# The first stage of an adaLN transformer block: modulation sums moved to the tensor engine, and a new order of the first lists

## The chip, the cores and the metric

The kernel runs on one core of one Trainium2 chip. The metric is the device time of one execution in microseconds (us). Engines are named as the profile names them: PE is the tensor engine (PEld its weight loads), DVE the vector engine, ACT the scalar engine, POOL the GpSimd engine, and SP the engine whose queue issues the transfers between device memory and the chip's SBUF. PSUM is the memory that PE writes its sums to; it is used here in banks of 512 float32 columns.

## What is computed

A block with adaptive layer norm: one conditioning row c gives six modulation rows, two of which (a shift `sa` and a scale `1 + ca`) act on the normalised input of the attention. The inputs are x (2048 rows of 576), c (one row of 576), `w_mod` (576 by 3456), the attention's `wqkv` and `wo`, and the feed-forward weights `w1` and `w2`, all float32. There are 32 heads of 18, and the feed-forward layer has 4608 columns.

```
mod = (silu(c) @ w_mod).reshape(1, 6, 1, 576)
sa, ca, ga, sb, cb, gb = (mod[:, i] for i in range(6))
h = layernorm(x) * (1 + ca) + sa
x = x + ga * attention(h, wqkv, wo)     # 32 heads of 18
h = layernorm(x) * (1 + cb) + sb
x = x + gb * (silu(h @ w1) @ w2)
```

## The kernel before

**Numbers in two parts.** Each large float32 product is computed from operands that are split into a high part (`fp32r`) and the rest, the low part. A product is made of three passes, high times high, high times low and low times high, for each of the four full slices of 128 of the 576 columns (kt 0 to 3). The last 64 columns (kt 4) hold the high part in one half of the partitions and the low part in the other, so two passes do there. This makes 14 matmuls for one sum; the names `hTh`, `hTl` (the transposed, modulated h), `wqh`, `wql` (a slice of the weights of q or k) and `wv` (those of v) are such parts.

**Two stages.** `start_tasks` writes the first stage, which ends at about 157 us in the profile; a planned main part follows with the attention and the feed-forward layer. The first stage is a list scheduler: each piece of work is a `Task` with an engine (P for PE, A for ACT, V for DVE, G for POOL, D for a transfer on SP's queue), an assumed duration, the tasks it depends on, a priority, and the buffers of rings that it takes and frees. `Start.run` steps through an assumed time and lets each free engine take the ready task of the smallest priority. The order in which tasks are taken is the order in which the instructions are written to each engine's queue; on the chip each queue runs strictly in that order, and each instruction waits for the data it needs.

**What the first stage does.** The rows of x come in 16 tiles of 128, in four groups of four (g 0 to 3). For a group: the tiles are loaded (`x_load`, L1368, 576 columns each, in a ring of eight buffers `xt`); `stats` takes mean and variance on DVE (L434, L435); `rstd_a`, `rstd_b` and `rstd_c` make the reciprocal deviation for the four tiles together, with a power on POOL (L1391) and five small operations on DVE (L1396 to L1400); `apply` normalises the tile in place on ACT (L1405); `dup` copies its last 64 columns once more behind the 576 on POOL (L1408), so that the fifth slice is 128 wide; `T` transposes slice kt of the four tiles on PE into one PSUM bank `psT` (L1413, four transposes), out of a ring of three banks; `out_T` reads the bank on ACT and applies scale and shift (`mod_out`, L459) into an SBUF tile `etmp`; `mod_hi` rounds `etmp` to the high part on DVE (L462, the CAST); `mod_lo` subtracts to the low part on POOL for even kt and on DVE for odd (L466, L468).

Then come the products: `single` (L1479) writes the 14 matmuls of one sum, in three parts of 6, 6 and 2. For k and q of a group (`psqk`, 512 columns) ACT takes the high part out of PSUM (L666) and DVE the low (L670), and both are stored to device memory (`kscr`, `qscr`); for v (`psv`, 288 columns) ACT copies the sum into `vst` (L1532), which is stored to `vscr`. Singles take turns on two PSUM banks, the rings f and v. Later products of the stage are written in pairs (`pair`, L539).

**The modulation.** c is loaded to all 128 partitions as a row, and silu(c) is made of it into `sbc` (L1355 on ACT, L1356 and L1357 on DVE). `w_mod`'s first two column blocks come transposed as five tiles `wm` of 128 by 1152 (`wf_load`, L1361). For each tile t, `mod_dot` takes two dot products with `sbc` on DVE (L567, 576 columns each, with the sum read out after each) and adds 1 to the scale (L572). The results stand in `modc`, one column for each t and kind; `out_T` of slice kt needs the two columns of t = kt. `aux` hands out one of three PSUM banks of the ring a; in the first stage it is used for the slots of the attention that are computed ahead (L890).

**Weights.** The weights of k and q come through a ring `raw` of two buffers, are rounded on ACT (L621) and subtracted on POOL (L626); the five tiles of v's weights come through the same ring (L616), are rounded on ACT (L1451) and subtracted on POOL (L1460), and take the buffers `wm` of the modulation when these are free.

## Time and profile before

| what | value |
|---|---|
| time, median of 3 runs | 2353.95 us (2350.65, 2353.95, 2354.07) |
| profiled execution, its own time | 2355.56 us |
| its span | 2353.8 us |
| PE busy in the span | 2293.4 us, 97% |
| DVE, ACT, POOL busy | 75%, 63%, 30% |
| first matmul starts | 17.63 us |
| first stage's last product, PE | 157.1 us |

The profile is of one execution. The difference of 1.8 us between its time and its span lies outside what the trace shows. A row of the timeline gives the start, the duration, the engine, the line, the operation with its output and inputs, and, in brackets, how long the engine was idle before and who released it. "x17" stands for 17 instructions in a row.

### The profile page before, as it was taken

The page shows a single profiled execution, that of the slowest core. Times are in us where ns is not written, and L with a number is a line of the kernel's source. Part 1 is how long each engine was busy: PE and PEld are TensorE (multiplying, and loading weights), DVE is VectorE, ACT ScalarE, POOL GpSimd, SP SyncE. Part 2 cuts the span into 40 slices and gives each one's busy share as a digit, 9 for nine tenths or more (in the row PEclk, how much of TensorE's full clock was granted, in tenths as well). Part 3 has the DMA queues.
Part 4 walks back from the last instruction along what each step waited for, and adds up shares of the span by engine and source line. Part 5 has one row for each costly group of instructions (what it writes and reads, how often), then busy time and mean ns, then how long its engine had stood idle before and what let it go on. Part 6 is the DMA issues. An engine that isn't in the chain of part 4 may idle for free.

```text
span 2353.8 us, 52121 instructions
## 1 busy us (share of the span) xinstructions
PE 2293.4 (97%) x19844; PEld 1580.8 (67%) x19844; DVE 1768.1 (75%) x3089; ACT 1473.9 (63%) x2710; POOL 712.2 (30%) x873
## 2 busy tenths in 40 slices
PE   5999999999899999999999999999999999999999
PEld 4874444444576767776677777776677767678998
DVE  7768899997788888877888878878887787344333
ACT  4337777776477777766677777766777677732221
POOL 5103333315656666675211111112211111110000
PEclk9999999999899999999999999999999999999999
DMA  7465555546456666666555555554645554345653
GB/s 243 154 194 175 168 168 168 184 151 209 157 192 219 222 222 214 218 207 227 206 171 171 183 176 167 166 181 141 224 165 164 194 184 174 115 152 196 221 201 114
DMA packets 201474, 433.01 MB, mean 184 GB/s; under 512 B 31362, under 2 KB 67618, under 8 KB 201226
## 3 DMA queue, kind: packets, MB, share of 16 engines
q1 hardware_dynamic: 201226, 429.68, 55.1%
q8 instruction: 158, 2.59, 0.5%
q14 instruction: 90, 0.74, 0.1%
HBM read 338.54 MB, written 86.33 MB: 181 GB/s over the span
## 4 chain that ended last, share of the span: by engine, by line
PE 86%; DVE 6%; DMA 3%; ACT 2%; issue 1%; POOL 1%; SPq 0%; DVEq 0%; ACTq 0%; POOLq 0%
PE ps L539 26%; PE psv L979 18%; PE psa L890 14%; PE ps L533 10%; PE psb L942 8%; PE psqk L654 3%; DVE mx L892 2%; PE psv L539 2%; DMA qt<-qscr 1%; PE psp L539 1%; PE psv L1479 1%; DMA raw<-in_w 1%; PE psqk L539 1%; PE psqk L1479 1%; PE psp L533 1%
## 5 line engine op out<-in xcount | busy, mean ns | idle before, releaser
L892 DVE TENSOR_REDUCE mx<-psa 128x1 f32<-128x512 f32 x2048 | 1329.2, 684 | 293.4 <-PE psb L942 165.2
L944 ACT ACTIVATE pt<-psb 128x512 f32<-128x512 f32 x2048 | 1148.4, 599 | 477.5 <-PE psb L942 303.8
L942 PE MATMUL psb<-qt,kb 56*128 56x512 f32 x2048 | 744.9, 421 | 3.5 <-ACT pt L944 3.5
L890 PE MATMUL psa<-ka,qt 54*128 54x512 f32 x2016 | 734.4, 418 | 11.9 <-DVE mx L892 9.3
L890 PEld LDWEIGHTS psa<-ka,qt 54*128 54x128 f32 x2016 | 348.6, 186 | 306.3 <-DVE mx L892 170.1
L979 PE MATMUL psv<-pt,vt 128*32 128x512 f32 x4096 | 510.1, 604 | 0.3 <-ACT ov L983 0.3
L539 PE MATMUL ps<-w2t,g 64*128 64x288 f32 x4992 | 412.5, 293 | 3.0 <-POOL w2t L775 1.6
L539 PEld LDWEIGHTS ps<-w2t,g 64*128 64x128 f32 x4992 | 384.4, 185 | 44.1 <-DVE x L1096 6.0
L942 PEld LDWEIGHTS psb<-qt,kb 56*128 56x128 f32 x2048 | 352.2, 186 | 26.4 <-ACT pt L944 15.7
L539 PE MATMUL ps<-hh,w1t 64*128 64x512 f32 x1944 | 352.9, 395 | 0.0
L1241 POOL TENSOR_TENSOR g<-etmp,g 128x512 fp32r<-128x512 f32 x108 | 137.4, 1292 | 386.6 <-ACT g L1240 349.4
L979 PEld LDWEIGHTS psv<-pt,vt 128*32 128x32 f32 x4096 | 102.3, 109 | 210.6 <-issue 202.5
L539 PEld LDWEIGHTS ps<-hh,w1t 64*128 64x128 f32 x1944 | 194.8, 186 | 43.1 <-ACT etmp L1237 3.4
L1103 POOL TENSOR_TENSOR x<-x,gt 128x288 f32<-128x288 f32 x116 | 93.1, 802 | 385.8 <-ACT gt L1102 385.4
L539 PE MATMUL ps<-hl,w1t 64*128 64x512 f32 x864 | 177.7, 392 | 0.0
L1096 DVE TENSOR_TENSOR x<-ps,x 128x288 f32<-128x288 f32 x184 | 83.3, 453 | 106.5 <-PE ps L533 71.5
L533 PE MATMUL ps<-w2t,g 128*128 128x288 f32 x960 | 130.8, 296 | 2.9 <-POOL g L1241 1.4
L533 PEld LDWEIGHTS ps<-w2t,g 128*128 128x128 f32 x960 | 128.6, 188 | 5.6 <-POOL g L1241 1.9
L1237 ACT ACTIVATE eq<-ps 128x512 f32<-128x512 f32 x36 | 21.6, 600 | 146.3 <-PE ps L533 146.3
L533 PE MATMUL ps<-hh,w1t 128*128 128x512 f32 x360 | 106.8, 390 | 0.5 <-DVE hh L468 0.5
L539 PEld LDWEIGHTS ps<-hl,w1t 64*128 64x128 f32 x864 | 88.8, 187 | 15.0
L1238 DVE SCALAR_TENSOR_TENSOR etmp<-etmp 128x512 f32<-128x512 f32 x108 | 74.6, 730 | 12.1 <-ACT etmp L1237 11.2
(150 smaller groups left out, 2138.8 us busy)
## 6 DMA issues: line engine op xcount, KB each, us to landing
w1t<-w1s SPq DMA_DIRECT2D x108, 640.0 KB
w2t<-w2s SPq DMA_DIRECT2D x108, 576.0 KB
kb<-kscr SPq DMA_DIRECT2D x512, 108.0 KB
ka<-kscr SPq DMA_DIRECT2D x504, 108.0 KB
w1s<-w1t SPq DMA_DIRECT2D x36, 640.0 KB
w2s<-w2t SPq DMA_DIRECT2D x36, 576.0 KB
vt<-vscr SPq DMA_DIRECT2D x32, 608.0 KB
qt<-qscr SPq DMA_DIRECT2D x128, 108.0 KB
```

The costliest lines, as they stand in the source:

```text
L533: mm(self.ps[late], lhsT=lhsT, rhs=rhs, start=(i == 0), stop=(i == self.n - 1))
L539: done = mm(self.ps[g], lhsT=lhsT[rows], rhs=rhs[rows], start=(s == 0), stop=(s == self.end))
L654: mm(qk_ps[0], lhsT=w[b][:, kt, :], rhs=(hTl if a else hTh)[:, kt, n * 512:(n + 1) * 512], start=(i == 0), stop=(i == 13))
L890: mm(ps, lhsT=t["q"][64 * j:64 * j + 54, hp, stt * P:(stt + 1) * P], rhs=t["a" if ("a", kc, hp) in t else "b", kc, hp][64 * j:64 * j + 54, ...
L892: return lambda: nc.vector.tensor_reduce(t["mx"][:, 2 * j + hp, stt, kc:kc + 1], ps, axis=AX.X, op=ALU.max)
L942: state["pe"] = mm(ps, lhsT=t["b", kt // 4, hp][64 * e:64 * e + 56, kt % 4 * P:(kt % 4 + 1) * P], rhs=t["q"][64 * e:64 * e + 56, hp, :], s ...
L944: nc.scalar.activation(t["P"][kt, hp][:, e, :], ps, AF.Exp, scale=SCALE)
L979: mm(t["ps"][32 * h:32 * h + 32, :], lhsT=t["v"][:, c0:c0 + 32], rhs=t["P"][kt, h // 2][:, h % 2, :], start=(kt == 0), stop=(kt == NKT - 1 ...
L1096: nc.vector.tensor_add(c["x1"][j][:, hs], ps, c["x1"][j][:, hs])
L1103: nc.gpsimd.tensor_add(c["x1"][j][:, hs], c["x1"][j][:, hs], t)
L1238: nc.vector.scalar_tensor_tensor(t, t, 1.0, u, op0=ALU.add, op1=ALU.mult)
L1241: (nc.vector if last else nc.gpsimd).tensor_tensor(g[:, 1, :], t, f(g[:, 0, :]), op=ALU.subtract)
```

## The change

- silu(c) is also made as a column: a small input `ccol` (128 by 6) is loaded first, and three small operations make `sc` of it. The row `sbc`, which the main part uses, is still made, but late (priorities 8.7 and 9).
- The ten dot products on DVE are gone. `mod_sum(t)` writes ten plain float32 matmuls of one column each on PE (five for the shift, five for the scale), with 128 by 128 slices of `w_mod` as weights, into a bank `psd` of the ring a. `mod_put(t)` is one small DVE operation that adds 0 and 1 to the two columns and stores them to `modc`. `w_mod`'s five tiles are laid out anew on the host; their size is the same.
- The high part of h is taken straight from the PSUM bank: `mod_hi_ps` is a DVE operation with scale and shift that reads `psT`, beside ACT's `out_T`, which reads it too. The CAST from `etmp` is gone. The low part waits for both.
- x is stored with its last 64 columns doubled, 640 wide. The copies on POOL are gone; loads and `apply` are 640 wide. Two of group 0's four `apply` are on DVE (`apply_v`).
- Singles take turns over the rings f, a, v, a: five banks in place of two. v's weights have a ring `rv` of four buffers of their own. The low parts of all weights wait, in the list, for group 0's norm.
- The list's rules change: some DVE tasks carry a flag `port`, and such a task and a task of POOL are not taken together; `RATE` is 340e3 for 320e3; transfers begin at 1.3. Several priorities and durations change.

```diff
-    RATE = 320e3
+    RATE = 340e3
+    FIRST = 1.3
...
+                if t.port and at <= now:
+                    held = min(held, t.prio)
+                at = max(at, free[t.eng], port if t.eng == "G" else free["G"] if t.port else 0.0)
...
+                if t.port and free["G"] > now or e == "G" and (port > now or t.prio > held):
+                    continue
+                if e == "V" and not t.port and t.prio > held and now + t.dur > free["G"] + 0.3:
+                    continue
...
+    def mod_hi_ps(kt, hi_dst, ps):
+        nc.vector.tensor_scalar(hi_dst, ps, modc[:, 1, kt:kt + 1], modc[:, 0, kt:kt + 1], op0=ALU.mult, op1=ALU.add)
...
-    def dot(w, dst):
-        return nc.vector.scalar_tensor_tensor(w, w, 1.0, sbc, op0=ALU.mult, op1=ALU.mult, accum_out=dst)
-
-    def mod_dot(i, t_, w):
-        ins = dot(w, modc[:, i, t_:t_ + 1])
-        if i % 2:
-            nc.vector.tensor_scalar_add(modc[:, i, t_:t_ + 1], modc[:, i, t_:t_ + 1], 1.0)
-        return ins
...
+        t = dma(20e3, lambda: nc.sync.dma_start(cc, ccol), prio=0)
+        t = add("A", 1.5, lambda: nc.scalar.activation(sc, cc, AF.Tanh, scale=0.5), [t])
+        t = add("V", 0.15, lambda: nc.vector.scalar_tensor_tensor(sc, sc, 1.0, cc, op0=ALU.add, op1=ALU.mult), [t], 0)
+        sc_t = add("V", 0.15, lambda: nc.vector.tensor_scalar_mul(sc, sc, 0.5), [t], 0)
...
+        def mod_sum(t_):
+            ps = d["ms", t_] = aux([P, 512], "psd")
+            for i in range(2):
+                for n in range(KT):
+                    c0, k_ = (256 * n + P * i, n) if n < 4 else (1024, 4 + i)
+                    mm(ps[:, i:i + 1], lhsT=d["wf", t_][:, c0:c0 + P], rhs=sc[:, k_:k_ + 1], start=(n == 0), stop=(n == KT - 1))
+
+        def mod_put(t_):
+            nc.vector.tensor_tensor(modc[:, 0:2, t_], d["ms", t_][:, 0:2], onec, op=ALU.add)
...
-            dots.append([add("V", 0.95 + 0.15 * i, lambda i=i, t_=t_: mod_dot(i, t_, d["wf", t_][:, i, :]), [t, sbc_t], 3, free=k) for i in range(2)])
+            k, ka = tok("wm"), tok("a")
+            t = dma(590e3, lambda t_=t_: wf_load(t_), prio=2 + 0.01 * t_, take=k)
+            t = add("P", 1.2, lambda t_=t_: mod_sum(t_), [t, sc_t], 3, take=ka, free=k, mode="full")
+            dots.append([add("V", 0.15, lambda t_=t_: mod_put(t_), [t], 1.5, free=ka)])
...
-            a_ = [add("A", 0.8, lambda i=4 * g + j: apply(i), [t], p - 0.5) for j in range(4)]
-            d_ = [add("G", 0.3, lambda i=4 * g + j: dup(i), [a_[j]], p - 0.5) for j in range(4)]
+            a_ = [add("A", 0.8, lambda i=4 * g + j: apply(i), [t], p - 0.5) if g or j % 2 == 0 else
+                  add("V", 0.58, lambda i=4 * g + j: apply_v(i), [t], 1.9) for j in range(4)]
...
-                hi = add("V", 0.6, lambda g=g, kt=kt: mod_hi(hl(g, kt)[0], d["e", g, kt]), [t], p - 0.4)
+                hi = add("V", 0.72, lambda g=g, kt=kt: mod_hi_ps(kt, hl(g, kt)[0], d["T", g, kt]), [tT] + dots[kt], p - 0.4, free=kb)
...
-            ring = "fv"[count[0] % 2]
+            ring = RINGS[count[0] % len(RINGS)]
```

The order of the instructions, at the places where it matters below. First PE, from its first instruction: `psT` are group 0's transposes, `psqk` its product of k, `psd` the new sums. Before:

```order
L1413 MATMUL psT<-ident,xt 128x128 x20
L1479 MATMUL psqk<-hTh,wqh 128x512
L1479 MATMUL psqk<-hTh,wql 128x512
L1479 MATMUL psqk<-hTl,wqh 128x512
L1479 MATMUL psqk<-hTh,wqh 128x512
L1479 MATMUL psqk<-hTh,wql 128x512
L1479 MATMUL psqk<-hTl,wqh 128x512
L1479 MATMUL psv<-wv,hTh 128x288 x2
```

and after:

```order
L1383 MATMUL psd<-sc,wm 128x1 x30
L1439 MATMUL psT<-ident,xt 128x128 x12
L1383 MATMUL psd<-sc,wm 128x1 x10
L1439 MATMUL psT<-ident,xt 128x128 x8
L1383 MATMUL psd<-sc,wm 128x1 x10
L1511 MATMUL psqk<-hTh,wqh 128x512
L1511 MATMUL psqk<-hTh,wql 128x512
L1511 MATMUL psqk<-hTl,wqh 128x512
```

The five groups of ten sums stand among the transposes of group 0, all ahead of the first product; the products of k and q now run one behind the other, and those of v, which stood between the parts of k, come after both.

Then DVE, from the last small operation of group 0's norm (`nm`) on. Before:

```order
L1400 SCALAR_TENSOR_TENSOR nm<-mv,rs 128x4
L567 SCALAR_TENSOR_TENSOR wm,modc<-wm,sbc 128x576 x2
L572 TENSOR_SCALAR modc<-modc 128x1
L567 SCALAR_TENSOR_TENSOR wm,modc<-wm,sbc 128x576 x2
L572 TENSOR_SCALAR modc<-modc 128x1
L567 SCALAR_TENSOR_TENSOR wm,modc<-wm,sbc 128x576 x2
L572 TENSOR_SCALAR modc<-modc 128x1
L462 CAST hTh<-etmp 128x512
L567 SCALAR_TENSOR_TENSOR wm,modc<-wm,sbc 128x576 x2
L572 TENSOR_SCALAR modc<-modc 128x1
```

and after:

```order
L1425 SCALAR_TENSOR_TENSOR nm<-mv,rs 128x4
L1386 TENSOR_TENSOR modc<-psd,onec 128x2
L1434 TENSOR_SCALAR xt<-xt,rs,nm 128x640 x2
L1386 TENSOR_TENSOR modc<-psd,onec 128x2 x2
L475 TENSOR_SCALAR hTh<-psT,modc 128x512 x3
L1386 TENSOR_TENSOR modc<-psd,onec 128x2
L475 TENSOR_SCALAR hTh<-psT,modc 128x512
L482 TENSOR_TENSOR hTl<-etmp,hTh 128x512
L1386 TENSOR_TENSOR modc<-psd,onec 128x2
L475 TENSOR_SCALAR hTh<-psT,modc 128x512
```

Eight of the ten dot products stood here behind the norm, with the first CAST among them; now there are five additions of two columns (`modc<-psd`), which wait for PE, two normalisations, and the high parts from `psT`.

Last POOL, from the power of group 0's norm to the first low parts. Before:

```order
L1391 TENSOR_TENSOR r_175<-ve,mhalf 128x4
L626 TENSOR_TENSOR wql<-raw,wqh 128x640
L1460 TENSOR_TENSOR wv<-raw,wv 128x576
L1408 COPY xt<-xt 128x64 x4
L1460 TENSOR_TENSOR wv<-raw,wv 128x576
L466 TENSOR_TENSOR hTl<-etmp,hTh 128x512
L1460 TENSOR_TENSOR wv<-raw,wv 128x576
```

and after:

```order
L1416 TENSOR_TENSOR r_183<-ve,mhalf 128x4
L633 TENSOR_TENSOR wql<-raw,wqh 128x640
L482 TENSOR_TENSOR hTl<-etmp,hTh 128x512 x2
L633 TENSOR_TENSOR wql<-raw,wqh 128x640
L484 TENSOR_TENSOR hTh<-etmp,hTh 64x512
L1492 TENSOR_TENSOR wv<-rv,wv 128x576 x2
L1416 TENSOR_TENSOR r_395<-ve,mhalf 128x4
```

The four copies and the low parts of v's weights are gone from between the norm and the low parts of h; v's come behind them.

From the last v products of the first stage on, PE's order is the same in both kernels, and behind the first stage the other engines differ by one or two rows that change places.

## Rows read from the trace of the kernel before

**Rows 1.** Windows by stretch: start, end, length, busy time by engine (instructions), clock, DMA.

```profile
core 0: us, PE busy (x) PEld busy (x) DVE busy (x) ACT busy (x) POOL busy (x), PEclk, DMA share, GB/s
0.00:5.00 5.00, 0.00 (x0) 0.00 (x0) 0.06 (x1) 1.28 (x1) 1.11 (x10) 1.00 0.58 118
5.00:17.60 12.60, 0.00 (x0) 0.00 (x0) 10.91 (x28) 3.08 (x5) 4.38 (x4) 1.00 0.97 356
17.60:25.10 7.50, 6.68 (x23) 4.85 (x23) 7.36 (x19) 6.31 (x9) 6.46 (x7) 1.00 0.78 263
25.10:45.00 19.90, 15.93 (x73) 13.18 (x73) 16.98 (x45) 8.34 (x14) 11.54 (x12) 0.83 0.65 208
45.00:60.00 15.00, 13.71 (x70) 11.24 (x68) 11.03 (x28) 9.03 (x15) 7.91 (x10) 0.89 0.68 235
60.00:157.10 97.10, 96.43 (x982) 84.94 (x982) 65.39 (x106) 25.10 (x51) 13.67 (x12) 1.00 0.53 171
```

**Rows 2.** Waits of PE from 17 to 160 us: total us, times, longest.

```profile
PE psT L1413 <- ACT xt L1405: 20.1, 8, 17.6
PE psqk L1479 <- DVE hTh L462: 1.5, 1, 1.5
```

**Rows 3.** Timeline of the start, all engines: start, duration, engine, line, operation.

```profile
11.34 0.74 ACT L621 ACTIVATE wqh<-raw 128x640 fp32r<-128x640 f32 x1 [5.07 <-DMA raw<-in_wqkv]
...
11.47 0.75 DVE L567 SCALAR_TENSOR_TENSOR wm<-wm,sbc 128x576 f32<-128x576 f32 x1
11.64 1.46 POOL L1391 TENSOR_TENSOR r<-ve,mhalf 128x4 f32<-128x4 f32 x1 [10.01 <-DVE ve L1387]
...
13.08 1.53 POOL L626 TENSOR_TENSOR wql<-raw,wqh 128x640 fp32r<-128x640 f32 x1
13.14 1.49 DVE L1396 TENSOR_TENSOR t<-r 128x4 f32<-128x4 f32 x1
...
14.67 1.32 DVE L1397 TENSOR_TENSOR t<-t,ve 128x4 f32<-128x4 f32 x1
...
16.62 3.14 ACT L1405 ACTIVATE xt<-xt,nm,rs 128x576 f32<-128x576 f32 x4 [2.42 <-DVE nm L1400]
...
17.63 0.45 PE L1413 MATMUL psT<-ident,xt 128*128 128x128 f32 x1 [17.63 <-ACT xt L1405]
```

**Rows 4.** Timeline of PE, transposes of group 0 and of group 1.

```profile
19.82 3.89 PE L1413 MATMUL psT<-ident,xt 128*128 128x128 f32 x17 [0.28 <-ACT xt L1405]
...
43.57 1.47 PE L1413 MATMUL psT<-ident,xt 128*128 128x128 f32 x12
```

**Rows 5.** Weight loads of the tile psm (ten float32 matmuls, later in the kernel): ns min/median/max.

```profile
L610 PEld LDWEIGHTS psm<-dg,full x20: 183/188/189, 291.9 to 436.8; 128*128 128x128 f32 x16, 64*128 64x128 f32 x4
```

**Rows 6.** The page's costliest groups: two weight loads, 128 and 32 columns wide.

```profile
L890 PEld LDWEIGHTS psa<-ka,qt 54*128 54x128 f32 x2016 | 348.6, 186 | 306.3 <-DVE mx L892 170.1
...
L979 PEld LDWEIGHTS psv<-pt,vt 128*32 128x32 f32 x4096 | 102.3, 109 | 210.6 <-issue 202.5
```

**Rows 7.** Windows around the stretches of low clock, columns as in Rows 1.

```profile
24.70:28.10 3.40, 1.88 (x7) 1.05 (x8) 3.30 (x8) 1.35 (x2) 1.97 (x2) 1.00 0.83 273
28.10:31.50 3.40, 3.40 (x12) 2.78 (x11) 3.40 (x3) 0.68 (x1) 2.97 (x3) 0.52 0.62 233
34.90:38.30 3.40, 2.70 (x11) 2.70 (x12) 3.30 (x11) 0.37 (x1) 2.54 (x2) 0.52 0.57 202
48.50:52.00 3.50, 2.21 (x10) 1.31 (x9) 3.43 (x8) 3.50 (x7) 3.42 (x4) 1.00 0.94 340
52.00:55.40 3.40, 3.40 (x10) 2.59 (x9) 2.95 (x10) 0.13 (x1) 1.97 (x5) 0.52 0.51 169
```

**Rows 8.** Groups by line and shape, 0 to 157 us: busy us, mean ns, idle before.

```profile
L459 ACT ACTIVATE etmp<-psT,modc 128x512 f32<-128x512 f32 x20 | 14.7, 778 | 2.2 <-DVE modc L572 1.3 <-PE psT L1413 0.7
...
L462 DVE CAST hTh<-etmp 128x512 fp32r<-128x512 f32 x20 | 12.3, 632 | 2.8 <-ACT etmp L459 2.8
...
L670 DVE TENSOR_TENSOR qkhl<-psqk,qkhl 128x512 fp32r<-128x512 f32 x12 | 7.9, 682 | 7.4 <-ACT qkhl L666 7.4
```

More of the change, by code (lines that the diff above doesn't have):

```diff
@@ L48 @@
 XTB = 8
+RVB = 4
+WVP, VOP, RINGS = 5, 4.5, "fava"
 ETB = 4
@@ L231, with __init__ @@
 class Task:
-    def __init__(self, eng, dur, fn, deps, prio, take, free, lag, mode):
+    def __init__(self, eng, dur, fn, deps, prio, take, free, lag, mode, port):
         self.eng, self.dur, self.fn, self.deps, self.prio = eng, dur, fn, [d for d in deps if d], prio
         self.take, self.free, self.lag, self.mode = take, free, lag, mode
+        self.port = port
         self.end = None
@@ L255, in __init__, with add @@
         self.taken = {r: [] for r in rings}
-    def add(self, eng, dur, fn, deps=(), prio=0, take=(), free=(), lag=0.0, mode="half"):
-        t = Task(eng, dur, fn, deps, prio, list(take), list(free), lag, mode)
+    def add(self, eng, dur, fn, deps=(), prio=0, take=(), free=(), lag=0.0, mode="half", port=False):
+        t = Task(eng, dur, fn, deps, prio, list(take), list(free), lag, mode, port)
         for k in t.free:
@@ L287, in run @@
     def run(self):
-        now, mode = 0.0, "half"
+        now, mode, port = 0.0, "half", 0.0
         free = {e: 0.0 for e in "PAVGD"}
+        free["D"] = self.FIRST
         todo = list(self.tasks)
@@ L298, in run @@
                     continue
-                at = max(at, free[t.eng])
+                if t.port and at <= now:
+                    held = min(held, t.prio)
+                at = max(at, free[t.eng], port if t.eng == "G" else free["G"] if t.port else 0.0)
                 if at > now + 1e-9:
@@ L316, in run @@
                 t.end = free[e] = now + dur
+                if t.port:
+                    port = t.end
                 for k in t.free:
@@ L393, in tile_adaln_block @@
 @with_exitstack
-def tile_adaln_block(ctx: ExitStack, tc: tile.TileContext, x, wqkv, wo, w1, w2, c, wfirst, wcol, out):
+def tile_adaln_block(ctx: ExitStack, tc: tile.TileContext, x, wqkv, wo, w1, w2, c, ccol, wfirst, wcol, out):
     nc = tc.nc
@@ L1335, in start_tasks @@
     def start_tasks(st):
-        S0 = Start({"b": 3, "f": 1, "v": 1, "a": 3, "xt": XTB, "wm": KT, "et": ETB, "vst": VSB, "qk": QKB, "raw": 2, "wq": 2})
+        S0 = Start({"b": 3, "f": 1, "v": 1, "a": 3, "xt": XTB, "wm": KT, "rv": RVB, "et": ETB, "vst": VSB, "qk": QKB, "raw": 2, "wq": 2})
         add, dma = S0.add, S0.dma
@@ L1445, in w_parts, with wv_load @@
             a = add("A", 0.74, lambda: d.update({("wh", key): hi_part(d["raw", key])}), [t], prio, take=kw)
-            b = add("G", 1.6, lambda: d.update({("wl", key): lo_part(d["raw", key], d["wh", key])}), [a], prio, free=kr)
+            b = add("G", 1.6, lambda: d.update({("wl", key): lo_part(d["raw", key], d["wh", key])}), [a, norm0], prio, free=kr)
             return kw, [a, b]
+        def wv_load(kt):
+            d["rv", kt] = st.tile([P, D], F32, name="rv", bufs=RVB)
+            nc.sync.dma_start(d["rv", kt], wqkv[:, kt, 2 * D:3 * D])
         def wv_hi(kt):
@@ L1475, in part @@
                 if n == 0:
-                    d["s", key] = (psV if ring == "v" else psF).tile([P, 512], F32, tag=ring, name="ps" + key[0])
+                    d["s", key] = {"v": psV, "f": psF, "a": psA}[ring].tile([P, 512], F32, tag=ring, name="ps" + key[0])
                 for i in range(14)[PARTS[n]]:
@@ L1570, in out @@
                     v_out(get(), hf, 2 * u + j)
-                outs.append(add("A", 0.42, out, [t] + outs, prio, take=kv if j == 0 else (), free=kb))
+                outs.append(add("A", 0.42, out, [t] + outs, VOP if prio < 9.8 else prio, take=kv if j == 0 else (), free=kb))
             v_stored.append(dma(311e3, lambda: v_store(hf, u), outs, prio, free=kv))
@@ L1760 @@
     wm = np.asarray(inputs["w_mod"]).reshape(D, 6, D)
-    cols = [_rows(wm[:, m].T) for m in range(6)]
-    wfirst = np.stack([cols[0], cols[1]], axis=2).transpose(1, 0, 2, 3)
-    wcol = np.stack([cols[m] for m in (3, 4, 2, 5)])
+    wcol = np.stack([_rows(wm[:, m].T) for m in (3, 4, 2, 5)])
+    wf = np.concatenate([wm[:, :2], wm[:, :2, 512:]], axis=2)
+    top = wf[:512].reshape(4, P, 2, KT, P).transpose(3, 1, 0, 2, 4).reshape(KT, P, 1024)
+    rest = wf[512:].reshape(64, 2, KT, P).transpose(2, 1, 0, 3).reshape(KT, P, P)
+    wfirst = np.concatenate([top, rest], axis=2)
+    ccol = np.zeros((P, KT + 1), np.float32)
+    cv = np.asarray(inputs["c"]).reshape(D)
+    ccol[:, :4] = cv[:512].reshape(4, P).T
+    ccol[:64, 4] = ccol[64:, 5] = cv[512:]
     arr = {
-        "x": x,
+        "x": np.concatenate([x, x[:, 512:]], axis=1),
         "wqkv": wqkv,
```

56 lines of the change are left out of this document (31 added, 25 removed).

## The prediction

> **What bounds the kernel now.** I read the windows by stretch first [rows 1]. PE is the engine to watch: from 60 us on it works 96.43 of 97.10 us, and the planned part behind 157.1 us keeps its order. So the change can give or take only what it does to the moment, now 157.1 us, at which PE ends the first stage. Up to there PE is idle 17.60 + 0.82 + 3.97 + 1.29 + 0.67 = 24.35 us. The waits [rows 2] say for what: 20.1 us for the normalised x, 17.6 of them ahead of the first transpose. The timeline [rows 3] shows why that first wait is so long. The power on POOL starts at 11.64, but the first two of the small DVE operations behind it took 1.49 and 1.32 us beside POOL's subtraction of `wql` (13.08 to 14.61), and `apply` began at 16.62.
>
> A second loss is the clock [rows 7]: the granted clock is 0.52, PE's lower level of 1.2 GHz, in 28.1 to 31.5, 34.9 to 38.3 and 52.0 to 55.4, each behind a stretch with idle time (1.88 busy of 3.40 and 2.21 of 3.50 are shown). PE's 3.40 + 2.70 + 3.40 = 9.5 us there would take about half at the higher level: some 4.6 us are lost. The early column reads 1.00 up to 25.1 us, but there the durations tell more [rows 4]: 17 transposes in 3.89 us are 0.229 each in group 0, and 12 in 1.47 us are 0.1225 in group 1. PE began at its lower level and stayed there through its first six microseconds of work.
>
> **The change, part by part.** The base is the profiled execution, 2355.56 us, which is 1.6 above the median of the three runs; I take that off at the end.
>
> *PE starts earlier.* The column of c costs next to nothing and comes first. Ahead of the first sum stand four tiles of x (0.328 MB each, now 640 wide) and one of `w_mod` (0.59 MB), 1.90 MB. The first 5 us moved 118 GB/s, 0.59 MB, and then 356 GB/s [rows 1]: 8.7 us. In the kernel before, 2.39 MB stood up to the first `raw`, by this 10.1 us; it was used at 11.34 [rows 3], so landing takes 1.3 more. The first sum can start at 10.0 us; the next tiles follow every 1.65 us.
>
> The norm is no longer late: `wql` is loaded three tiles later and the dots are gone, so I expect `nm` near 12.6 and the four normalised tiles near 14.5, from the same operations at their undisturbed lengths. The transposes stand behind the third sum and need not wait. So 10.0 us of idle time stand in place of 17.6, and most of the later 6.75 us falls too: when PE comes later or has more to do, loads, norms and weights are ahead of it. I allow S = 1 us of idle time behind the first sum (0 to 3). The gain is 24.35 - 10.0 - 1.0 = 13.35 us.
>
> *What the sums cost on PE.* This is the large term, and no row before shows a matmul of one column. In [rows 5] ten plain float32 matmuls have 20 weight loads: each takes two passes. Ten sums are thus 20 loads of 128 columns, and with one moving column there is nothing to hide a load behind. The price of a load: rows of 128 and of 32 columns last 186 and 109 ns [rows 6], so 96 columns are 77 ns and 128 are 0.103 us, at the higher level; twice that, 0.205, at the lower. The transposes, which also load 128 float32 columns each, give 0.1225 and 0.229 [rows 4], as an upper end. A `mod_sum` is then 2.05 to 2.45 us at the higher level and 4.1 to 4.6 at the lower, where the list assumes 1.2.
>
> Which level? PE starts from rest, and the nearest thing to such a row of loads that the trace shows, the transposes of group 0 from rest, went through at the lower level from the first to the last [rows 4]. I take that for all five sums, the middle 4.4 each: +22.0 us (20.5 to 22.9).
>
> *The clock later.* Before the first product PE would have worked without a gap, but its first products would still run at the lower level; I put that at the length of one of the drops, 3.4 us, a loss of 1.6. The three later drops have no idle time left to follow: 4.6 - 1.6 = 3.0 us gained.
>
> *The high part from PSUM.* A DVE operation on 512 columns from PSUM (`qkhl`) takes 682 ns [rows 8], against 632 for the CAST on the mean, many of them stretched beside POOL. About equal for DVE. What the trace of before does not show is ACT and DVE reading the same bank. The bound below is nothing (both read at once); above, one waits for the other and a bank costs 0.78 + 0.68 us [rows 8] before it is free, 7.3 us for a group's five. Taking the upper end: for group 0 PE's sums cover it, and for the others PE has some 11 us of products a group. It stays inside S.
>
> The Trainium skill, "PSUM — Partial Sum Buffer", section "PSUM bank collisions raise a hardware error", speaks against the gain hoped for here: two engines may not read one bank in the same partitions at once, reads against reads included, so the compiler puts them one behind the other. No row of the kernel before shows it. By it the sum is the one just made; with free reading S would be about 0.5 less.
>
> *The rest.* Copies of 64 columns leave POOL; x's loads and `apply` are 11% longer, covered by products from group 1 on, and priced in the 10.0 us for group 0. Five banks for singles remove the waits of PE for `qkhl` and `vst`, already counted as idle time. The order of k, q and v costs PE nothing by itself.
>
> *Sum:* -13.35 + 22.0 - 3.0 = +5.65: 2361.2 for the profiled execution, 2359.5 at the level of the median. Sums at 20.5 and S = 0 give 2357; sums at 22.9 and S = 3 with no clock gain give 2365.5.
>
> **The rivals.** *The clock rises under the sums.* If the first sum is slow (4.4) and the level rises behind it, four take 2.25: 13.4 us. The transposes save 20 x 0.107 = 2.1, and the full 4.6 of the clock comes back; PE reaches group 1 sooner, so S = 2: -12.35 + 13.4 - 2.1 - 4.6 = -5.65, 2348.3; with S from 1 to 5 it is 2347 to 2351. For it: every drop followed idle time, and the sums leave none; the clock stood at 1.00 from 24.7 on, right behind transposes and the first products [rows 7]. Against it: the transposes alone did not bring it there [rows 4].
>
> *The sums are nearly free.* If a pass costs what its column costs, or 60 ns as the list's 1.2 us implies, the last tile of `w_mod` is the limit: 4.59 MB, landed near 17.5. First product near 21; idle time 10.4 + 2; sums 6; clock 3: -11.95 + 6 - 3 = -9, near 2345. Against it stand the load rows [rows 6]. The Trainium skill, "TensorE: Matmul & The Clock Gate", section "Back-to-back issue gap", puts a matmul of 1 to 64 columns at about 60 cycles, a floor of some 25 ns; by that alone a group of 20 passes is 0.5 us, which is this rival. The same page's section on LDWEIGHTS prices 128 columns at 107 ns; the 0.103 us from the rows agrees with this one, and so I follow the load.
>
> *A new wait behind fast sums.* In DVE's queue the statistics of group 1 stand behind the last sum's high part. From the end of that sum: 0.15 + 0.68 + 1.2 for the low part, 4 x 1.03 statistics, 0.2, 1.2 power, 1.0, and 3.8 for four `apply`, 12.3 us; PE's products until group 1's transposes are 28 x 0.23 + 40 x 0.13 = 11.6 us at the higher level. That is even; with the low parts stretched beside POOL, as `t` was [rows 3], the transposes of groups 1 to 3 wait 2 us more each, S = 8, and a drop of the clock comes back: -6.35 + 13.4 - 2.1 - 4.6 + 1.6 = +1.95, near 2356. It decides only where the sums are fast.
>
> **How the numbers follow.** Sums at the lower level 0.45, at 2359.5, 2357 to 2365.5: the forecast. The clock rises 0.29. Nearly free 0.13. New waits 0.13. What a measurement of this kernel can tell from no change is about 0.2%, 4.7 us: 2349.2 to 2358.7. The forecast splits 0.29 slower, 0.16 same; the clock case 0.17 faster, 0.12 same; nearly free is 0.12 faster, 0.01 same; new waits 0.01 faster, 0.08 same, 0.04 slower. So faster 0.30, same 0.37, slower 0.33. The forecast's own range is 2357 to 2365.5; to hold 8 in 10 the range must reach into the clock case: 2345.5 to 2364.
>
> **What would show it.** First matmul at about 10 us, `nm` near 12.6. Group after group of ten sums at 4.1 to 4.6 us, the first `psqk` near 37 us, where it was at 23.4 before; at 27 the clock rose, at 21 the sums were cheap. The windows from 38 to 60 us should be full; idle time there is the new wait. The last v product ends near 162 in place of 157. I am wrong if a `mod_sum` takes under 3 us, or if PE stands after the products of group 0.

## The result and the profile after

| | kernel before | changed kernel |
|---|---|---|
| median | 2354.07 us (22 runs) | 2359.1 us (22 runs) |
| lowest to highest | 2348.33 to 2359.1 | 2352.49 to 2365.12 |
| ratio of the two, 95% interval | | 1.0021 [1.0013, 1.0029] |
| span of the profiled execution | 2353.8 us | 2357.5 us |
| first matmul starts | 17.63 us | 10.41 us |
| first product starts | 23.4 us | 35.79 us |
| PE ends the first stage | 157.1 us | 162.6 us |

The change makes the kernel 0.21% slower, about 5 us. The forecast was 2359.5 us. PE ends the first stage 5.5 us later; behind it the order of PE's work is the same as before.

The timeline of PE in the changed kernel, from its first instruction (start, duration, line, output and inputs, count):

```profile
10.41 12.93 PE L1383 MATMUL psd<-sc,wm 128*128 128x1 f32 x60 [10.41 <-DMA wm<-in_wfirst]
23.20 2.80 PE L1439 MATMUL psT<-ident,xt 128*128 128x128 f32 x12
25.80 4.26 PE L1383 MATMUL psd<-sc,wm 128*128 128x1 f32 x20
29.92 1.95 PE L1439 MATMUL psT<-ident,xt 128*128 128x128 f32 x8
31.66 4.26 PE L1383 MATMUL psd<-sc,wm 128*128 128x1 f32 x20
35.79 0.77 PE L1511 MATMUL psqk<-hTh,wqh 128*128 128x512 f32 x1
...
39.77 0.63 PE L1511 MATMUL psqk<-hTh,wqh 128*128 128x512 f32 x1
...
40.77 0.40 PE L1511 MATMUL psqk<-hTh,wqh 128*128 128x512 f32 x1
```

Each group of ten sums stands as 20 rows. The first sixty take 12.79 us from start to start (10.41 to 23.20), 0.213 each, and the later twenties 4.12 each between the transposes. The transposes among them have the pitch of group 0 before [rows 4]: 12 take 2.60 us, 0.217 each. All of this is PE's lower level, and the first products still run at it: rows of 0.63 us up to 40 us, then 0.40. A transpose moves 128 columns behind its load and a matmul of a sum moves one, and both have about the same pitch. The weight loads of the sums, by their tile (duration min/median/max in ns):

```profile
L1383 PEld LDWEIGHTS psd<-sc,wm x100: 286/333/337, 10.4 to 35.5; 128*128 128x128 f32 x100
L1383 PE MATMUL psd<-sc,wm x100: 212/352/353, 10.4 to 35.6; 128*128 128x1 f32 x100
```

A hundred loads of 128 columns for fifty matmuls of one column: two passes each, as in [rows 5]. Now the windows that answer to [rows 1] (start, end, length, busy by engine and instructions, clock, DMA), and the waits of PE up to 200 us (total, times, longest):

```profile
10.41:35.80 25.39, 25.39 (x121) 25.39 (x121) 8.71 (x16) 6.14 (x8) 6.74 (x5) 1.00 0.63 224
35.80:60.00 24.20, 21.28 (x114) 18.25 (x115) 20.19 (x48) 14.65 (x23) 14.17 (x11) 1.00 0.47 146
60.00:80.00 20.00, 18.78 (x114) 15.94 (x113) 14.81 (x34) 11.77 (x18) 6.38 (x5) 1.00 0.83 275
80.00:100.00 20.00, 18.65 (x139) 15.79 (x139) 12.01 (x18) 7.70 (x14) 6.97 (x5) 1.00 0.57 172
100.00:162.00 62.00, 61.87 (x752) 60.53 (x750) 46.56 (x76) 11.04 (x26) 3.13 (x2) 1.00 0.55 177
```

```profile
PE psd L1383 <- DMA wm<-in_wfirst: 10.4, 1, 10.4
PE psT L1439 <- ACT etmp L472: 2.1, 2, 1.2
PE psT L1439 <- DVE hTh L475: 2.0, 3, 1.0
...
PE psv L1511 <- DVE qkhl L677: 1.2, 1, 1.2
```

PE has no gap in the 25.4 us of sums and transposes. But it is idle again where I expected it full: 2.92 us up to 60, 1.22 up to 80, 1.35 up to 100. About four of these are waits of transposes (`psT`) for a bank, which have no counterpart in [rows 2]; there the transposes waited for x. The three low stretches of [rows 7] are gone: from 40 us on the clock reads 1.00 up to 162 us. (Ahead of 40 us the column reads 1.00 as well, though the rows have the pitch of the lower level; the last section comes back to this.)

The new wait in the timeline of ACT, DVE and PE, at group 1's transposes:

```profile
51.98 1.45 ACT L472 ACTIVATE etmp<-psT,modc 128x512 f32<-128x512 f32 x2 [0.19 <-PE psT L1439]
...
52.79 0.81 DVE L475 TENSOR_SCALAR hTh<-psT,modc 128x512 fp32r<-128x512 f32 x1 [1.64 <-ACT etmp L472]
...
53.61 0.78 ACT L472 ACTIVATE etmp<-psT,modc 128x512 f32<-128x512 f32 x1
...
53.66 0.66 PE L1439 MATMUL psT<-ident,xt 128*128 128x128 f32 x4 [0.63 <-DVE hTh L475]
...
55.50 1.52 DVE L475 TENSOR_SCALAR hTh<-psT,modc 128x512 fp32r<-128x512 f32 x2
...
56.36 0.66 PE L1439 MATMUL psT<-ident,xt 128*128 128x128 f32 x4 [0.98 <-DVE hTh L475]
```

ACT reads the first bank into `etmp` (the first of two, up to 52.76); DVE's `hTh` begins at 52.79, after 1.64 us of waiting for just that; and at its end, 53.60, the bank is free and the fourth slice's transposes start. The two reads of a bank stand one behind the other, where before only ACT read it. This is what the Trainium skill, "PSUM — Partial Sum Buffer", section "PSUM bank collisions raise a hardware error", says of two readers, and the trace agrees. The read of DVE takes 0.81 us here, a little more than the 0.68 that I took from [rows 8].

The fifth slice waits longer, 0.98 us, and for one reason more. ACT had read the second bank by 53.43, but DVE's read of it starts only at 55.50: the small operations of the next group's norm stand ahead of it in DVE's queue. So the second reader costs its own time and also the time that it spends in its queue.

### The profile page after: what moved, and what is told of

It is laid out like the page before. It is cut to its first block, busy times and chain, and to the rows that moved or that the text cites. A ratio compares the mean times of both kernels' runs of the same rounds, so it can differ in the third digit from the quotient of the medians.

```text
span 2357.5 us, 52278 instructions
## 1 busy us (share of the span) xinstructions
PE 2306.3 (98%) x19944; PEld 1599.5 (68%) x19944; DVE 1765.7 (75%) x3075; ACT 1471.6 (62%) x2709; POOL 705.4 (30%) x857
## 4 chain that ended last, share of the span: by engine, by line
PE 86%; DVE 5%; DMA 4%; ACT 2%; POOL 2%; issue 1%; SPq 0%; DVEq 0%; ACTq 0%; POOLq 0%
PE ps L555 26%; PE psv L986 18%; PE psa L897 14%; PE ps L549 10%; PE psb L949 8%; PE psqk L661 3%; DVE mx L899 2%; PE psv L555 2%; DMA raw<-in_w 1%; PE psp L555 1%; PE psd L1383 1%; PE psqk L555 1%; PE psqk L1511 1%; PE psv L1511 1%; DMA qt<-qscr 1%
```

## The experiments

Ratios are to the kernel before, each against runs of it on the same chip. The changed kernel stands at 1.0021; one thousandth is 2.35 us.

| kernel | ratio, 95% interval | PE ends the first stage, us |
|---|---|---|
| changed kernel | 1.0021 [1.0013, 1.0029] | 162.6 |
| e_two: sums over two of five slices | 0.9972 [0.9963, 0.9981] | 151.3 |
| e_warm: constant products first | 0.9991 [0.9978, 1.0003] | 155.3 |
| e_dots: dots on DVE | 1.0001 [0.9990, 1.0011] | 154.7 |
| e_etmp: high part from SBUF | 1.0005 [0.9993, 1.0016] | 157.9 |
| f_warm_etmp: both | 0.9982 [0.9970, 0.9994] | 155.8 |
| f_dots_etmp: dots on DVE, high part from SBUF | 0.9966 [0.9955, 0.9978] | 149.4 |
| f_hyb2: two sums on PE, six dots on DVE, high part from SBUF | 0.9954 [0.9937, 0.9970] | 147.8 |
| f_fv: two banks for singles | 1.0048 [1.0033, 1.0063] | 163.6 |
| g_hyb2_warm: f_hyb2, constant products first | 0.9969 [0.9956, 0.9982] | 147.5 |
| g_hyb1: one sum on PE, eight dots on DVE | 0.9963 [0.9951, 0.9974] | 147.1 |
| g_dup: f_dots_etmp, x 576 wide, copies on POOL | 0.9972 [0.9959, 0.9985] | 150.0 |
| g_noport: f_dots_etmp without the port flag | 0.9998 [0.9985, 1.0010] | 153.1 |

**Do the loads of the sums cost the time? (e_two)**

```diff
-                for n in range(KT):
+                for n in range(2):
...
-                    mm(ps[:, i:i + 1], ..., start=(n == 0), stop=(n == KT - 1))
+                    mm(ps[:, i:i + 1], ..., start=(n == 0), stop=(n == 1))
```

> The changed kernel, but each sum of the modulation takes only the first two of its five slices of 128 (so 40 weight loads in place of 100; the modulation is not the reference's). Nothing else is moved. Theory: the loads at PE's lower level are what costs the time. Then a group of sums takes 1.7 us in place of 4.26, the first product of k starts near 24 us in place of 35.8, the first stage ends 9 to 12 us earlier, and the time is near 2348. Rival: the waits of PE in groups 1 to 3 (5.6 us of idle time from 36 to 100 us) hold the end; then they grow, and no more than 3 to 5 us come back (2354 to 2356).

PE's timeline of this kernel:

```profile
10.64 5.25 PE L1383 MATMUL psd<-sc,wm 128*128 128x1 f32 x24 [10.64 <-DMA wm<-in_wfirst]
15.75 2.80 PE L1439 MATMUL psT<-ident,xt 128*128 128x128 f32 x12
18.34 1.71 PE L1383 MATMUL psd<-sc,wm 128*128 128x1 f32 x8
19.91 1.95 PE L1439 MATMUL psT<-ident,xt 128*128 128x128 f32 x8
21.65 1.71 PE L1383 MATMUL psd<-sc,wm 128*128 128x1 f32 x8
```

A group of eight loads takes 1.71 us, the same 0.21 each. Sixty loads fewer at 0.213 are 12.8 us; the first product starts at 23.2 in place of 35.8, the first stage ends 11.3 us earlier, and 0.0049 or 11.5 us come off the time. Little behind the sums took the gain back, 1.3 of 12.6 us. So the theory holds: the loads lie on the path, at about 0.9 us of time for each us of loads.

**Why the lower level? (e_warm)**

```diff
+        def warm():
+            ps = psF.tile([P, 512], F32, tag="f", name="psw")
+            for _ in range(24):
+                mm(ps[:, :P], lhsT=full, rhs=full, start=True, stop=True)
+
+        kf = tok("f")
+        add("P", 6.0, warm, (), -1, take=kf, free=kf)
```

> The changed kernel with 24 plain float32 products of 128 columns of a constant ahead of the first sum, in PE's idle time from about 2 to 10 us; their sums are used by nobody. Theory A: the sums are slow because PE starts from rest; once at the upper level it stays there while it has no idle time. Then a group of sums takes 2.1 to 2.4 us, the transposes 0.12 each, the first product starts near 24 us, and the time is near 2348. Theory B: a row of weight loads with one column each does not hold the upper level. Then the first one or two groups are fast and the others take 4.26 again, the first product starts near 32 us, and the time falls by 2 to 4 us, to about 2356.

PE's timeline, and then windows through the sums and transposes (the count behind PE is its rows, the number ahead of the DMA's two is the granted clock):

```profile
1.13 7.84 PE L1377 MATMUL psw<-full 128*128 128x128 f32 x48 [1.13 <-POOL full L580]
9.85 10.39 PE L1391 MATMUL psd<-sc,wm 128*128 128x1 f32 x60 [0.87 <-DMA wm<-in_wfirst]
```

```profile
10.00:12.00 2.00, 2.00 (x20) 2.00 (x20) 0.82 (x5) 0.16 (x1) 0.81 (x1) 1.00 1.05 381
...
14.00:16.00 2.00, 2.00 (x11) 2.00 (x11) 0.00 (x0) 0.46 (x1) 1.46 (x1) 0.50 1.05 362
...
22.60:25.00 2.40, 2.40 (x23) 2.40 (x22) 1.69 (x3) 1.39 (x2) 1.27 (x1) 0.94 0.10 37
...
27.00:29.50 2.50, 2.50 (x13) 2.50 (x14) 2.17 (x2) 0.01 (x1) 1.54 (x1) 0.50 0.93 352
```

With 7.84 us of products ahead, the first sums run at the upper level: 20 rows in the 2 us from 10 to 12, 0.10 each. Then the level falls in the middle of the sums, with PE without a gap: 11 rows in 2 us at a clock of 0.50. In the transposes from 20.1 on it is low, rises behind them (0.94 from 22.6), and falls again in the last sum. Theory A, and with it the reason that I gave (start from rest), is only half of it. The first fall, near 12.6 us, comes 2.8 us behind a gap of 0.87 us, so alone it could be put down to that gap. The second, near 26.3, cannot: PE had had no gap since 9.85, and since the rise near 22.9 it had done a sum, eight transposes and the start of the next sum. In both PE was in a row of loads with one column each, as theory B has it. The first product starts at 29.6, and 0.0030 or 7 us come off, more than the 2 to 4 I wrote for B, since 6 us of PE time were won and not 4.

**The dots back on the vector engine (e_dots)**, all else as changed:

```diff
...
-            t = add("P", 1.2, lambda t_=t_: mod_sum(t_), [t, sc_t], 3, take=ka, free=k, mode="full")
-            dots.append([add("V", 0.15, lambda t_=t_: mod_put(t_), [t], 1.5, free=ka)])
+            dots.append([add("V", 0.95 + 0.15 * i, lambda i=i, t_=t_: mod_dot(i, t_, d["wf", t_][:, i, :]), [t, sbc_t], 3, free=k) for i in range(2)])
...
```

> The changed kernel with the modulation taken back to the vector engine (the row of silu(c) early, ten dot products, the weights laid out as before), and all else as changed: high parts from PSUM, x with doubled columns, five banks, the new list rules. Theory: the sums on PE alone made the change slow, and the other parts are worth something. Then the first product of k starts near 23 us, PE waits some 4 us less behind it than the kernel before does, and the time is 2348 to 2352. Rival: the other parts cost as much as they give; then it is within 2 us of the kernel before, 2352 to 2356.

The ratio is 1.0001, a median of 2354.85 us: the rival's range holds it, and the theory's does not. The first product starts at 26.50 and not near 23. The timelines of PE and DVE show two things, one early and one at the end of the first stage:

```profile
24.02 2.24 DVE L475 TENSOR_SCALAR hTh<-psT,modc 128x512 fp32r<-128x512 f32 x3
...
24.88 1.97 PE L1428 MATMUL psT<-ident,xt 128*128 128x128 f32 x8 [5.92 <-DVE hTh L475]
```

```profile
150.04 5.39 PE L906 MATMUL psa<-ka,qt 54*128 54x512 f32 x9
```

The fourth slice's transposes of group 0 wait 5.92 us for the bank of the first, because the high part now reads that bank, and in DVE's queue it stands behind all ten dot products, up to 24.02 us. And the list put nine slots of the attention together at the end, where PE goes at the pace of DVE's maxima (`mx`): 4.6 us for nine matmuls. The second is an accident of the list's order. So this kernel says little of what the other parts are worth; f_dots_etmp, below, says more.

**The high part from SBUF again (e_etmp)**

```diff
-                hi = add("V", 0.72, lambda g=g, kt=kt: mod_hi_ps(kt, hl(g, kt)[0], d["T", g, kt]), [tT] + dots[kt], p - 0.4, free=kb)
+                hi = add("V", 0.6, lambda g=g, kt=kt: mod_hi(hl(g, kt)[0], d["e", g, kt]), [t], p - 0.4)
```

> The changed kernel with the high part taken from the SBUF tile again (the CAST) in place of PSUM; the list orders the work with the duration of before. Theory: the waits of the transposes for the bank (4.1 us, for the low part's ACT reader and the high part's DVE reader) come from the two readers of one bank that run one behind the other. Then these waits shrink to under 2 us and the time falls by 1 to 3 us. Rival: the CAST is stretched beside POOL and the chain over SBUF is longer; then the time is the same or up to 2 us more.

PE's waits of this kernel up to 170 us:

```profile
PE psqk L1511 <- DVE hTl L482: 1.7, 1, 1.7
...
PE psv L1511 <- POOL wv L1492: 1.1, 1, 1.1
...
PE psT L1439 <- ACT xt L1430: 0.2, 1, 0.2
```

The four us of waits for `etmp` and `hTh` at the transposes are gone (0.2 is left, for x); 1.7 for a low part and 1.1 for v's weights stand in their place. PE's idle time behind the first product falls from 5.62 to 3.3 us, 2.3 less, within the 1 to 3 that I wrote. The first stage ends 4.7 us earlier, but 1.0 of that is an earlier first sum (9.42 for 10.41), which the edit does not explain. The ratio falls by 0.0016, 3.8 us, with intervals that overlap, so the price of the second reader is a few us and no more exact than that. The theory held in kind. With both this edit and that of e_warm (f_warm_etmp):

> The changed kernel with both: 24 idle-time products of a constant ahead of the first sum, and the high part from the SBUF tile again. Theory: the two gains lie at different places (the rate of the loads before 30 us; the bank's two readers behind 50 us) and add up: 7.0 + 3.8 us less than the changed kernel, a ratio of about 0.9975 to the kernel before, 2348 us. Rival: both only bring PE to the same later wait (the norm of groups 1 and 2); then the ratio is about 0.999, as with the first alone.

The ratio is 0.9982, where adding the two would give 0.9975 and the rival 0.999; the interval holds all three, so how far they add up stays open.

**What is left without sums and without the second reader (f_dots_etmp)**, the edits of e_dots and e_etmp together:

> The changed kernel with the dot products on the vector engine and the high part from the SBUF tile: what is left of the change is x with doubled columns, five banks, the buffers and the list rules. Theory: the wait of 5.9 us of the fourth transpose for a bank that the late high part still held is gone, PE has all of group 0 transposed by 20 us, the first product of k starts near 23 us, and the ratio to the kernel before is 0.997 to 0.9985 (2347 to 2350.5 us). Rival: the vector engine is the limit (dots, CASTs, statistics in one queue); the first product starts no earlier and the ratio stays at 1.000.

0.9966: 8 us faster than the kernel before, a little more than written. The 5.9 us wait is gone. But the first product starts no earlier than in the kernel before (23.4); it waits for DVE:

```profile
24.70 0.80 PE L1500 MATMUL psqk<-hTh,wqh 128*128 128x512 f32 x1 [3.84 <-DVE hTh L478]
```

So the start is DVE's, as the rival says, and the time falls all the same. Of the parts that are left I took back three, one at a time; the rest (two of the normalisations on DVE, the buffers of v's weights, the late low parts of the weights, the new rates and priorities) was not tried alone.

*Two banks (f_fv)*, from the changed kernel:

```diff
-WVP, VOP, RINGS = 5, 4.5, "fava"
+WVP, VOP, RINGS = 5, 4.5, "fv"
```

> The changed kernel with the singles on two banks again (rings f, v) in place of five. Theory: PE waits for the readers of these banks (the low part of k and q, the copies of v) as in the kernel before; the time is 1 to 4 us more than the changed kernel's, a ratio of 1.0025 to 1.004. Rival: behind the long sums the readers are never late; the time is the same within 1 us, a ratio of 1.002.

PE's waits up to 200 us:

```profile
PE psv L1511 <- DVE qkhl L677: 5.8, 3, 2.8
...
PE psT L1439 <- DVE hTh L475: 1.1, 2, 0.6
```

The ratio rises to 1.0048, and the wait for `qkhl`, 1.2 us in the changed kernel, is 5.8. In the changed kernel the five banks are worth some 6 us, more than the 1 to 4 that I wrote; with the intervals of both, 2 to 10. What they are worth with the dots on DVE was not tried. In this execution, the shortest of the four, the clock rose at the fourth sum, behind the first transposes:

```profile
24.95 2.34 PE L1383 MATMUL psd<-sc,wm 128*128 128x1 f32 x20
```

and the first product started at 31.8; the loss is behind that. Up to there PE's order is that of the changed kernel, where the same sum took 4.26. So the level under the sums is not the same in every execution: here it rose for a while and fell again in the fifth sum.

*The doubled columns (g_dup)*, from f_dots_etmp:

```diff
-            nc.sync.dma_start(d["x", i], x[i * P:(i + 1) * P, :])
+            nc.sync.dma_start(d["x", i][:, :D], x[i * P:(i + 1) * P, :D])
...
+            d_ = [add("G", 0.3, lambda i=4 * g + j: dup(i), [a_[j]], p - 0.5) for j in range(4)]
```

> The kernel with all dots on the vector engine and the high part from the SBUF tile, in which x is stored 576 wide again and POOL copies the last 64 columns (the rest as changed: five banks, buffers, list rules). Theory: the copies, 0.24 to 0.64 us each, hold the fifth transposes and POOL's low parts of group 0 by about 1 us, against loads and apply that are 10% shorter; the ratio is 0.9966 to 0.998, so the doubled columns are worth 0 to 3 us. Rival: the shorter loads win; the ratio is 0.9955.

0.9972 against 0.9966, with intervals that overlap: no difference that these runs can tell. The rival's 0.9955 lies outside the interval.

*The port flag (g_noport)*, from f_dots_etmp:

```diff
-..., [hi, t], p - 0.4, free=ke, port=on == "V")
+..., [hi, t], p - 0.4, free=ke)
```

> The kernel with all dots on the vector engine and the high part from the SBUF tile, with the flag for the shared port taken off the low parts, so that the list may place them beside POOL's work. Theory: the vector engine's low parts are stretched beside POOL's (1.65 in place of 0.69 us), the queue behind them is late by 1 us a group, and the ratio is 0.9975 to 0.9985. Rival: on the chip the queues meet anyway; the ratio stays at 0.9966.

The low parts on DVE in f_dots_etmp and then in this kernel (busy us, mean ns):

```profile
L482 DVE TENSOR_TENSOR hTl<-etmp,hTh 128x512 fp32r<-128x512 f32 x8 | 7.8, 990 | 0.0
```

```profile
L482 DVE TENSOR_TENSOR hTl<-etmp,hTh 128x512 fp32r<-128x512 f32 x8 | 10.4, 1296 | 0.3
```

They are 0.31 us longer on the mean beside POOL, 2.4 us in all; in f_dots_etmp two of the eight take over 1.7 us and the others about 0.7, in g_noport five take 1.65. The ratio rises by more, by 0.0032 or 7.5 us, and the first stage ends 3.7 us later; but this list, too, has nine slots in a row at the end, 4.6 us on PE:

```profile
148.52 5.38 PE L906 MATMUL psa<-ka,qt 54*128 54x512 f32 x9
```

So the stretch is shown, and what the flag is worth alone is not: the order of the slots is in the difference too.

**The modulation shared between PE and DVE (f_hyb2)**: the sums of slices 0 and 1 on PE, the dots of 2 to 4 on DVE, the row of silu(c) loaded behind the first two tiles of `w_mod`, the high part from SBUF.

```diff
...
+            if t_ < NPE:
+                ka = tok("a")
+                t = add("P", 4.2, lambda t_=t_: mod_sum(t_), [t, sc_t], 3, take=ka, free=k, mode="full")
+                dots.append([add("V", 0.15, lambda t_=t_: mod_put(t_), [t], 1.5, free=ka)])
+            else:
+                dots.append([add("V", 0.8 + 0.15 * i, lambda i=i, t_=t_: mod_dot(i, t_, d["wf", t_][:, D * i:D * i + D]), [t, sbc_t], 3, free=k) for i in range(2)])
...
```

> The changed kernel with the work of the modulation shared: the sums of two of the five slices stay on PE, the dot products of the other three go back to the vector engine (the row of silu(c) is loaded behind the first two tiles of w_mod), and the high part comes from the SBUF tile. Theory: PE spends 8.5 us on sums at its lower level in place of 21.3, the vector engine 5 us in time that it has idle, the first product of k starts near 24 us and the ratio to the kernel before is 0.996 to 0.998 (2344.5 to 2349). Rival: the vector engine's queue delays group 0's CASTs and group 1's statistics; then the transposes of group 1 wait 3 us or more and the ratio is 0.999 to 1.001.

PE's timeline:

```profile
9.59 8.67 PE L1394 MATMUL psd<-sc,wm 128*128 128x1 f32 x40 [9.59 <-DMA wm<-in_wfirst]
18.12 4.26 PE L1454 MATMUL psT<-ident,xt 128*128 128x128 f32 x20
22.14 0.48 PE L1526 MATMUL psqk<-hTh,wqh 128*128 128x512 f32 x1
22.46 0.40 PE L1526 MATMUL psqk<-hTh,wql 128*128 128x512 f32 x1
```

The first sum fills the time in which PE would wait for x, and the second the time in which it would wait for DVE (with one sum, below, the transposes start at 13.59 and PE then waits). The vector engine does the rest while the transposes run, and the first product starts at 22.1, earlier than in any other of these kernels but one. The ratio is 0.9954 [0.9937, 0.9970], with a median of 2344.99 us in four runs: faster than the kernel before and than the changed one, but not told apart from f_dots_etmp, with no sum on PE, whose interval overlaps. With one sum on PE (g_hyb1: `NPE = 1` in place of 2, the row loaded behind the first tile), and with e_warm's edit on top (g_hyb2_warm):

> As the shared modulation, but one sum on PE and eight dots on the vector engine. Theory: PE is no longer the limit of the start; the vector engine ends its dots 1.7 us later (two more of 0.83), the CASTs and the first product follow it, and 1 to 2 us are lost against two sums: a ratio of 0.996. Rival: PE's 4.3 us saved count; the ratio is 0.994.

> The shared modulation (two sums on PE, six dots on the vector engine, high part from the SBUF tile) with 24 idle-time products of a constant ahead of the first sum. Theory: the upper level holds for the first 20 or 25 loads only, as in the run with these products alone; the two sums take 6.4 us in place of 8.5, but behind the transposes PE waits anyway for low parts (2.4 us), so 0 to 2 us are won: a ratio of 0.9945 to 0.9955. Rival: the transposes and first products are fast too, and 4 us are won, 0.9935.

they are 0.9963, as written, and 0.9969, more than written. The three intervals overlap, so which share is best isn't settled. With the high part from SBUF in all, the ratio is 1.0005 with five sums on PE (e_etmp), 0.9954 with two, 0.9963 with one and 0.9966 with none (f_dots_etmp): five cost 9 to 12 us, and between none, one and two these runs show no difference. With one sum, PE waits for DVE again:

```profile
9.33 4.39 PE L1394 MATMUL psd<-sc,wm 128*128 128x1 f32 x20 [9.33 <-DMA wm<-in_wfirst]
13.59 4.51 PE L1454 MATMUL psT<-ident,xt 128*128 128x128 f32 x20
22.94 0.80 PE L1526 MATMUL psqk<-hTh,wqh 128*128 128x512 f32 x1 [4.85 <-DVE hTh L478]
```

With products ahead, two sums take 5.7 us in place of 8.5, and PE then waits 2.3 us for a bank: the gain ends in a later wait, as the theory has it. The level of the first products differs as well: in f_hyb2 they run at the upper one (0.40 us), in g_hyb1 at the lower (0.63) up to 32 us, and in g_hyb2_warm, from 23.5 on, up to 29.4.

## Why the prediction was right, and where it wasn't

*The number.* 2359.5 was forecast and 2359.1 measured. That is closer than the working deserved: the forecast had a chance of 0.45, the range of 2345.5 to 2364 held gains as well as losses, and of the three outcomes I gave the largest chance, 0.37, to no change that can be told, and 0.33 to slower, which came. The start and the sums, the two largest terms, were right for the reasons given; the idle time was not.

*What bounds it.* That the time moves by what PE's end of the first stage moves is borne out: 157.1 to 162.6, 5.5 us, against 5.0 between the medians. In the profiled executions the spans differ by 3.7 only; single executions of one kernel differ by several us, and I don't read the difference of 1.8 us. Of the other twelve kernels, the end of the first stage and the ratio agree within 1.5 us in seven; in f_warm_etmp, g_hyb2_warm, e_dots, g_noport and f_fv they are 2.3 to 4.8 us apart, one execution against a median.

*The start.* First sum at 10.0, measured 10.41; `nm` near 12.6, measured 12.11. The four normalised tiles near 14.5 were not: ACT's two end at 14.0, but DVE's two stand behind the addition of the first sum. Timeline of DVE:

```profile
12.11 0.16 DVE L1425 SCALAR_TENSOR_TENSOR nm<-mv,rs 128x4 f32<-128x4 f32 x1
...
14.85 0.16 DVE L1386 TENSOR_TENSOR modc<-psd,onec 128x2 f32<-128x2 f32 x1 [2.58 <-PE psd L1383]
14.92 2.35 DVE L1434 TENSOR_SCALAR xt<-xt,rs,nm 128x640 f32<-128x640 f32 x2
```

They wait until 14.92 and take 2.35 us beside POOL's `wql`, in place of the 1.14 that the same two take in f_hyb2. I had not seen this wait in the order of DVE's queue. It cost nothing: the transposes started at 23.2, behind the third sum. One reading of [rows 3] was wrong: the second of the small operations that I saw stretched (14.67 to 15.99) stood beside POOL's next subtraction, that of `wv` (14.58 to 15.98), since that of `wql` had ended at 14.61. No term hangs on it.

*The sums.* 4.4 us each at the lower level, measured 4.12 to 4.26; 22.0 in all, measured 12.79 + 4.12 + 4.13 = 21.0 from start to start. Two passes for a plain float32 matmul, and a price set by the load and not by the column, came straight from [rows 5, 6], and the level from [rows 4]; the pitch of 0.213 us, the same as that of transposes with 128 columns (0.217), bears the price out. In e_warm the same loads at the upper level took 0.10 each, as the difference of the two load rows said (0.103). The rival of nearly free sums is out; so is the list's 1.2 us. The Trainium skill, "TensorE: Matmul & The Clock Gate", section "Back-to-back issue gap", gives a floor of about 25 ns for a matmul of up to 64 columns; here each one came with a load, and the pitch was 0.213 us.

*The level, the reason.* I took the lower level because PE started from rest, as the transposes before it. The level was right and the reason was short: in e_warm, with PE busy from 1.1 us on but for 0.87 us, the level still fell inside the sums, twice. The rival "the clock rises under the sums" is not what the profiled execution did. In f_fv, with the same order up to the first product, the level did rise, but behind transposes, and fell again in the last sum: the first product started at 31.8, where the rival had 27.

*Idle time behind the sums.* This is the term that was mis-sized: S = 1 us, at most 3, and it measured 2.92 + 1.22 + 1.35 + 0.13 = 5.62. PE did stand behind the products of group 0, which was one of my two signs of being wrong. I had seen the wait for the second reader of a bank, priced it at 7.3 us for a group, and then covered it with PE's products. It isn't covered where group 1's transposes stand between v products of 0.4 us: with three banks, the fourth slice waits for both readers of the first. And I had priced the read alone, not the place of the second reader in DVE's queue, behind the next group's norm. In e_etmp, without that reader, 2.3 of the 5.62 us are gone.

*Why the sum was right all the same.* The start gave 7.2 and the sums took 21.0; PE's end moved by 5.5; so the rest gave 8.3 us. I had 8.75 for it, 5.75 of idle time and 3.0 of clock. By the busy columns the idle time fell by 6.75 - 5.62 = 1.1 only, and the first products ran low for 4.6 us and not 3.4. But the busy columns understate a gap: in [rows 3] a lone transpose lasts 0.45 where 17 in a row have 0.229 each [rows 4].

The starts of PE's rows tell more. In an unbroken row a product of 512 columns follows the one before by 0.228 us at the upper level and 0.427 at the lower, one of 288 columns by 0.133 and 0.240, and a transpose by 0.109 and 0.213. For these three kinds, the time in the first stage beyond that pitch is about 13.3 us before and 8.4 after, 4.9 less; what the lower level adds to them is 6.9 before and 4.2 after, 2.7 less; the other 0.8 is in the products on half the array and the slots. So the two terms came out near their size, 4.9 for 5.75 and 2.7 for 3.0. But the first was a difference of two idle times that were both too small by about 7 us: 13.3 where I read 6.75, and 8.4 where I allowed 1. That these two errors took each other back is luck.

*The banks for singles.* I counted their gain as idle time of before (1.0 for `qkhl`); f_fv shows that, with this order of products, they are worth about 6 us. That stands inside the sum, and not by my working.

## What to carry to other kernels

A matrix times one vector on PE cost its weight loads here and not its columns: for plain float32, two loads of the full tile for each matmul, at about the pitch of transposes of the same tile (0.213 for 0.217 us at the lower level, 0.10 for 0.12 at the upper). Count that, and compare it with the vector engine's dots before moving them. A second reader of a PSUM bank lengthens the time until the bank is free, by its own read and by what stands ahead of it in its queue, and with few banks that comes back as a wait of PE. Work moved to an engine that is idle should fit into the time ahead of the first thing that the engine must do next: five sums did not, at a cost of 9 to 12 us. That one or two sums are better than none is not shown.

## What the runs showed of the hardware that I had not expected

PE's clock fell while PE had no gap at all. In e_warm it went from 20 rows in 2 us to 11, at a granted clock of 0.50, inside a row of loads with one column each, came back behind 12 transposes, and fell again in such loads near 26.3 us, with PE busy without a break since 9.85; in f_fv it rose and fell at the same places. In the other kernel with the start of e_warm (f_warm_etmp) it did not come back behind the transposes. The clock column of the windows read 1.00 in the changed kernel from 10 to 40 us, while the pitch of its rows (0.213 for a load, products of 0.63) was that of the lower level: there only the rows' times told the level. In e_warm, where it had once risen, the same pitch stands beside 0.50.
